# Modulation rows weighed on GpSimd, and a product order of its own at the start of units 2 to 14

## The chip, the cores and the metric

The kernel runs on one core of a Trainium2 chip. The metric is the device time of one execution in microseconds, as the median of several runs. Engines are named as the profile names them: PE (TensorE, with PEld for its weight loads), DVE (VectorE), ACT (ScalarE), POOL (GpSimd) and SP (SyncE, which here only issues DMAs).

## What is computed

A transformer block with adaptive layer norm, all in fp32: x is 2048 rows of 576 features. A condition vector c gives six rows of modulation, softmax attention with 32 heads of 18 features follows, then a gated feed-forward part with 4608 inner features.

```python
mod = (silu(c) @ w_mod).reshape(1, 6, 1, 576)
sa, ca, ga, sb, cb, gb = (mod[:, i] for i in range(6))
h = layernorm(x) * (1 + ca) + sa
q, k, v = split_heads(h @ wqkv)                  # 32 heads of 18
o = softmax(q @ k.T * 18 ** -0.5) @ v
x = x + ga * (merge_heads(o) @ wo)
h = layernorm(x) * (1 + cb) + sb
x = x + gb * ((sigmoid(h @ w_gate) * (h @ w_up)) @ w_down)
```

## The kernel before

**Stages.** First the layer norm and the projections of q, k and v (to about 240 us), then attention (to about 1600 us), then the feed-forward part. The change touches attention alone.

**Units and steps.** Attention runs over 32 units `u`. A unit is one half of the query rows (1024) and one pair of heads (`h` = 0, 1). It has 16 steps `kt`, one for each 128 keys. A step holds:
- four score products ("t", line 927): 128 keys by 512 queries, for two query chunks `c` and two heads, each followed by an exp on ACT (line 931) that takes the scores out of PSUM;
- four products for row maxima ("m", line 449, the generator `maxima`): 128 queries by 512 keys, for a unit that comes later. DVE reduces each (line 455). The order of the eight products of a block of 128 queries is in the table `MAXIMA`, as pairs (h, key chunk kc). In units outside `SINGLE` two of the eight are paired: product (0, 0) is made of the difference of two key chunks, ACT puts its relu into the tile `over` (line 458), and DVE later adds `over` to product (0, 1) and takes the maximum (line 460). The generator runs `LEAD` = 6 steps ahead, so that steps 0 and 1 of unit u make the fourth block (`qt` = 3) of unit u + 1;
- value products ("v", line 551, `values`): four products of 32 columns each, side by side, for the probabilities of two steps earlier. They sum into one PSUM tile `o` over a unit's 16 steps. A string such as "vmmttmmtvt" for even and "mtkttmwmmt" for odd steps gives the order; both calls of "v" fall into the even step.
- "k" (`taken`): after the last value product of a unit, ACT copies `o` to SBUF (line 565). That happens in step 1 of the next unit, and the next unit's first value product, in step 2, needs `o` free.
- "w": other work, in step 3 the four transposes of `outputs` (line 575), with a second ACT copy (line 590) and two POOL products (line 594). In step 13 `spread` writes the row maxima of a later unit into its query tile.

**What sets the order.** PE's order is the written one (`manual_schedule`). The other engines' orders are made by the framework's list scheduler when the program is built, so an instruction of theirs can be placed well ahead of where it is written. All score, maxima and helper products take their PSUM tiles from `bank()`, seven in rotation.

**Modulation.** `modulate(row, wm, pieces, takes)` makes two of the six rows at a time. `wm` holds five tiles of features (four of 128 and one of 64) by 2 x 576 columns of `w_mod`; `sc` is silu(c) by column. The weights of the products are `sc_b`, sc broadcast to 32 columns. For the later rows (`HALVES`) that is 5 x 2 x 2 = 20 products of 288 columns, summed over the five tiles; fp32 products have two rows in the profile, so 40 rows of line 124. Then DVE copies the sums to `row` (lines 130, 131), PE transposes it in three (line 142), and the results go to `mcol2` by DVE or to `ga_b` and `gb_b` by DMA (lines 148, 149). In unit 1 and in unit 3, after step 2, `load_mod` (lines 97, 98) loads the weights of two rows; after step 10 of the same unit `modulate` runs as a whole. The tiles `big`, `w0` and `w1` hold the weights and `row`.

**Others.** `downs` prepares `w_down` on POOL in the slots `w0` and `w1` (lines 826 to 848), one call every second step from step 64 (unit 4) to step 240 (unit 15); it needs `gb_b`.

Of the kernel before, what the change touches and what calls it, by code (L numbers as in the profile page):

```python
# [15 lines left out]
F32 = mybir.dt.float32  # L16
F32R = mybir.dt.float32r
AF = mybir.ActivationFunctionType
ALU = mybir.AluOpType
# [28 lines left out]

MAXIMA = ((1, 0), (0, 0), (1, 1), (0, 2), (1, 2), (0, 3), (0, 1), (1, 3))
SINGLE = (0, 1, 16, 17, 18, 19, 20, 27, 28, 29)  # L50
SIDES = ((0, 0), (0, 1), (1, 0), (1, 1))
TURNED = ((0, 1), (0, 0), (1, 1), (1, 0)), ((0, 1), (1, 1), (0, 0), (1, 0))
ORDERED = 7
# [5 lines left out]
def tile_block(ctx, tc, x_in, wqkv, wo, w_gate, w_up, w_down, c_in, w_mod, out):  # L59
# [41 lines left out]
    def ksize(t):  # L101
        return P if t < 4 else 64


    QUARTERS = (
        ((0, 0, 0, 384), (1, 0, 384, 192)), ((1, 192, DM, 64),),
    )
# [2 lines left out]
    def modulate(row, wm, pieces, takes):  # L110

        sc_b = row[:, 384:544].rearrange("p (t c) -> p t c", c=32)
        nc.vector.tensor_copy(sc_b, sc.unsqueeze(2).to_broadcast([P, 5, 32]))
        row = row[:, 0:384]
        pm = bank()
        for parts in pieces:
            for t in range(5):
                k = ksize(t)  # L120
                for v in range(2):
                    for g, to, f0, n in parts:
                        q = 32 * (2 * v + g)
                        nc.tensor.matmul(
                            pm[q : q + 32, to : to + n], sc_b[:k, t, :],
                            wm[t][:k, v * D + f0 : v * D + f0 + n],
                            start=t == 0, stop=t == 4, tile_position=(0, q),
                        )
        if pieces is HALVES:
            nc.vector.tensor_copy(row[:, 0:HALF], pm[:, 0:HALF])  # L130
            nc.vector.tensor_copy(
                row[:, HALF:384].rearrange("p (r c) -> p r c", c=32),
                pm[:, HALF - 32 : HALF].unsqueeze(1).to_broadcast([P, 3, 32]),
            )
        else:
            nc.vector.memset(row[:, 256:384], 0.0)
            nc.vector.tensor_copy(row[:, 0:256], pm[:, 0:256])
            for q in (0, 64):
                nc.vector.tensor_copy(row[q : q + 32, 256:384], pm[q : q + 32, 256:384])
        pt = bank()  # L140
        for b in range(3):
            nc.tensor.transpose(pt[:, b * P : (b + 1) * P], row[:, b * P : (b + 1) * P], ident)
        cols = pt[:, 0:384].rearrange("p (b q) -> p b q", q=P)
        for v, (dst, add) in enumerate(takes):
            if add is None:
                for g in range(2):
                    q = 64 * v + 32 * g
                    nc.sync.dma_start(gates[v : v + 1, g * HALF : (g + 1) * HALF], row[q : q + 1, 0:HALF])
                nc.sync.dma_start(dst, gates[v : v + 1, :].to_broadcast([P, D]))
            else:  # L150
                n = dst.shape[-1]
                nc.vector.tensor_scalar_add(dst[:, 0:3], cols[:, :, 64 * v], add)
                nc.vector.tensor_scalar_add(dst[:, 3:n], cols[:, 0 : n - 3, 64 * v + 32], add)
# [185 lines left out]
    with tc.tile_pool(name="ln", bufs=2) as ln:  # L339
        craw = early.tile([P, 5], F32, name="craw")  # L340
        nc.vector.memset(craw, 0.0)
        nc.sync.dma_start(craw[:, 0:4], c_in[0, 0:DM].rearrange("(t p) -> p t", p=P))
        nc.sync.dma_start(craw[0:64, 4:5], c_in[0, DM:D].rearrange("(p o) -> p o", o=1))
        nc.scalar.activation(sc, craw, AF.Sigmoid)
        nc.vector.tensor_mul(sc, sc, craw)

        def normalized(ch):
            xs = []
            for j in range(4):
                xt = ln.tile([P, 640], F32, name="x", bufs=8)  # L350
                nc.sync.dma_start(xt[:, :D], x_rows[:, ch * 4 + j, :])
                xs.append(xt)
            mv = ln.tile([P, 4, 2], F32, name="mv")
            rs = ln.tile([P, 4], F32, name="rs")
            for j, xt in enumerate(xs):
                ln_stats(ln, xt[:, :D], mv[:, j, :])
            ln_scales(ln, mv, rs)
            for j, xt in enumerate(xs):
                ln_apply(xt, xt[:, :D], mv[:, j, 0:1], rs[:, j : j + 1])
            return xs  # L360

        with tc.tile_pool(name="wmp", bufs=1) as wmp:
            zs = normalized(0)
            wm = wmp.tile([P, 5, 2 * D], F32, name="wm")
            wm = load_mod(wm[:, 0:4, :], wm[:, 4, :], 0)
            modulate(wmp.tile([P, 544], F32, name="mrow"), wm, QUARTERS, [(mcol[:, 1, :], 0.0), (mcol[:, 0, :], 1.0)])
        nc.gpsimd.memset(vaug, 1.0)
        wts = [load_qk([(0, P)]), load_qk([(D, P)])]
        with tc.tile_pool(name="wv0", bufs=1) as wvp:
            wv = load_v(wvp, 0)  # L370
            ln_transpose(ln, zs, hT, 0)
            zs = normalized(1)
            pls = []
            for ch in range(NCH):
                pls.append(project_qk([(wt, ch) for wt in wts]))
                if ch == 1:
                    key_differences(wvp, pls[0][:, :, 512:1024], pls[1][:, :, 512:1024], 0, P, 0)
                if ch + 1 < NCH:
                    ln_transpose(ln, zs, hT, (ch + 1) * 512)
                if ch + 2 < NCH:  # L380
                    zs = normalized(ch + 2)
                for t in (4 * ch, 4 * ch + 2):
                    project_v(wv, 0, t)
# [42 lines left out]
    def maxima():  # L426
# [4 lines left out]
        for u in range(UNITS):  # L431
# [5 lines left out]
            for i in range(8 * n):  # L437
                if last is not None and i == (9 if u == 1 else 8):
                    if u == 1:
                        spread(*last)  # L440
                    else:
                        state["spread"] = last
                qt = i // 8
                h, kc = MAXIMA[i % 8]
                rows = slice(64 * h, 64 * h + 3 * DH)
                paired = pairs and h == 0 and kc < 2
                at = NCH if paired and kc == 0 else kc
                sp = bank()
                nc.tensor.matmul(  # L449
                    sp, qs[rows, qt * P : (qt + 1) * P],  # L450
                    ks[rows, at * 512 : (at + 1) * 512], start=True, stop=True,
                )
                to = mx[:, h * n + qt, kc : kc + 1]
                if not paired:
                    nc.vector.tensor_reduce(to, sp, axis=AX.X, op=ALU.max)  # L455
                elif kc == 0:
                    over = small.tile([P, 512], F32, name="over", bufs=1)
                    nc.scalar.activation(over, sp, AF.Relu)
                else:
                    nc.vector.tensor_tensor_reduce(  # L460
                        out=over, in0=sp, in1=over, scale=1.0, scalar=LOWEST,
                        op0=ALU.add, op1=ALU.max, accum_out=mx[:, h * n + qt, 0:1],
                    )
                if i < 8 * n - 1:
                    yield
# [426 lines left out]
    for u in range(UNITS):  # L892
# [5 lines left out]
            Os.append(big.tile([P, 8, 640], F32, name="big"))  # L898
        for kt in range(NT):
            step = u * NT + kt  # L900
            turns["to"] = 64 + 4 * LEAD + 4 * (step + 1)
            kcols = slice(kt * P, (kt + 1) * P)
            plain = u in SINGLE
            sides = iter(SIDES if plain else TURNED[kt % 2])
            probs = [None] * 4
            for does in (("vtmmttmvtm", "tmttkwmtmm") if plain else ("vmmttmmtvt", "mtkttmwmmt"))[kt % 2]:
                if does == "m":
                    turn()
                elif does == "k":
# [21 lines left out]
                    state["exp"] = nc.scalar.activation(pr, sT, AF.Exp, scale=SCALE)  # L931
            pending.append((half, p, kt, probs))
            if u in (1, 3):
                if kt == 2:
                    a = big.tile([P, 8, 640], F32, name="big")
                    a = a.rearrange("p a b -> p (a b)")[:, 0 : 8 * D].rearrange("p (t c) -> p t c", t=4)
                    b = slots.tile([P, 2560], F32, name="w0")[:, 0 : 2 * D]
                    mods = load_mod(a, b, 1 + u // 2)
                    row = slots.tile([P, 2560], F32, name="w1")[:, 0:544]
                elif kt == 10 and u == 1:  # L940
                    modulate(row, mods, HALVES, [(ga_b, None), (mcol2[:, 1, :], 0.0)])
                elif kt == 10:
                    modulate(row, mods, HALVES, [(mcol2[:, 0, :], 1.0), (gb_b, None)])
            if 4 * NT <= step < FROM0 and step % 2 == 0:
                next(downs, None)
            if step == FROM0:
                for _ in downs:
# [471 lines left out]
```

## Time and profile before

| what | value |
|---|---|
| median of 3 runs | 2897.66 us (2895.02 to 2898.18) |
| profiled execution | 2895.19 us |
| its span, first to last instruction | 2893.2 us |
| PE busy | 2836.9 us |
| DVE, ACT, POOL busy | 2212.7, 1563.3, 644.6 us |
| products of the later modulation rows, L124, in units 1 and 3 | 2.74 us each, at 310.40 and 394.75 us |
| copies of `o` by ACT, L565 | 32, mean 608 ns |

A row of the chain of waits is "start us, length us, what ended last there"; "x8" is the number of instructions that are merged into it. In a timeline row stand start, length, engine, line, operation, output and inputs, and in brackets the idle time of the engine before it and what ended that. A row of the groups ends with busy us and mean ns, then idle us before them and who ended it.

### The profile page before, as it was taken

What the parts mean: (1) busy time and instruction counts of PE and PEld (TensorE: products, weight loads), DVE (VectorE), ACT (ScalarE), POOL (GpSimd) and SP (SyncE); (2) the same over time, 40 slices, a digit from 0 to 9 for tenths busy, and PEclk for the clock granted to TensorE, in tenths of its full rate; (3) what the DMA queues carried; (4) which work ended last, traced back from release to release, by engine and by line L of the source; (5) the groups of instructions that cost most, each with busy time, mean ns of one, the idle gap of its engine ahead of it and who ended that gap; (6) DMA issues with size and microseconds to landing.
All of it is one profiled execution on the core that took longest, in us unless ns stands there. A gap on an engine that the chain in (4) does not pass through costs nothing.

```text
span 2893.2 us, 46407 instructions
## 1 busy us (share of the span) xinstructions
PE 2836.9 (98%) x17141; PEld 1879.0 (65%) x17141; DVE 2212.7 (76%) x4055; ACT 1563.3 (54%) x2941; POOL 644.6 (22%) x829
## 2 busy tenths in 40 slices
PE   7999999999999999999999999999999999999998
PEld 5964333343444444444443788888888888888888
DVE  7287888888899988999983778888898555555555
ACT  2216889999987778998779322333333111111111
POOL 4023015444203111563101322222221100000000
PEclk9999999999999999999999999999999999999999
DMA  5344114333312111222215766667777845444453
GB/s 167 126 155 135 57 57 154 120 123 126 110 48 68 52 36 44 95 84 67 65 55 156 273 216 229 241 213 269 282 251 283 300 168 169 166 164 160 160 166 123
DMA packets 136386, 429.26 MB, mean 148 GB/s; under 512 B 19100, under 2 KB 55968, under 8 KB 123872
## 3 DMA queue, kind: packets, MB, share of 16 engines
q1 hardware_dynamic: 119664, 344.20, 35.2%
q0 software_dynamic: 16496, 82.10, 8.1%
q8 instruction: 135, 2.21, 0.3%
q14 instruction: 91, 0.75, 0.1%
HBM read 267.77 MB, written 157.95 MB: 147 GB/s over the span
## 4 chain that ended last, share of the span: by engine, by line
PE 89%; DVE 4%; ACT 4%; DMA 2%; issue 1%; SPq 0%; POOL 0%; DVEq 0%; POOLq 0%; ACTq 0%
PE x L1050 26%; PE o L551 17%; PE d L1096 15%; PE s L449 11%; PE s L927 11%; PE s L277 4%; ACT p L931 3%; PE s L688 2%; PE s L328 2%; DVE mx L455 1%; PE s L575 1%; DMA ws<-w 1%; DVE w L1040 0%; DVE Oa L1100 0%; DMA wm<-in_w_mod_dram 0%
## 5 line engine op out<-in xcount | busy, mean ns | idle before, releaser
L455 DVE TENSOR_REDUCE mx<-s 128x1 f32<-128x512 f32 x1696 | 1076.5, 684 | 122.2 <-PE s L449 108.4
L931 ACT ACTIVATE p<-s 128x512 f32<-128x512 f32 x2048 | 1068.8, 610 | 147.4 <-PE s L449 80.4
L449 PE MATMUL s<-k,q 54*128 54x512 f32 x1920 | 607.4, 450 | 13.0 <-ACT p L931 6.0
L551 PE MATMUL o<-p,vaug 128*32 128x512 f32 x4096 | 554.1, 606 | 0.4 <-ACT p L931 0.4
L927 PE MATMUL s<-q,k 56*128 56x512 f32 x1920 | 551.4, 425 | 0.7 <-DMA q<-mrows 0.2
L1096 PE MATMUL d<-wd,hh 128*128 128x288 f32 x2304 | 460.9, 295 | 3.0 <-DVE Oa L1100 2.8
L927 PEld LDWEIGHTS s<-q,k 56*128 56x128 f32 x1920 | 260.1, 186 | 293.5 <-DVE mx L455 183.8
L449 PEld LDWEIGHTS s<-k,q 54*128 54x128 f32 x1920 | 273.4, 184 | 250.3 <-ACT p L931 172.0
L1096 PEld LDWEIGHTS d<-wd,hh 128*128 128x128 f32 x2304 | 373.4, 188 | 9.7 <-DVE Oa L1100 3.7
L1050 PE MATMUL x<-k,w 128*128 128x512 f32 x1512 | 357.6, 391 | 2.4 <-ACT w L1031 2.4
L1100 DVE TENSOR_TENSOR Oa<-Oa,d 128x288 f32<-128x288 f32 x576 | 256.3, 454 | 134.2 <-PE d L1096 128.3
L1096 PE MATMUL d<-wd,hl 128*128 128x288 f32 x1152 | 340.3, 295 | 0.0
L1050 PEld LDWEIGHTS x<-k,w 128*128 128x128 f32 x1512 | 282.7, 188 | 59.3 <-ACT w L1031 2.6
L1050 PE MATMUL x<-big,w 128*128 128x512 f32 x1008 | 235.6, 390 | 0.7 <-DVE u L1338 0.7
L1050 PE MATMUL x<-w,w 128*128 128x512 f32 x1008 | 235.7, 390 | 0.0
L1096 PEld LDWEIGHTS d<-wd,hl 128*128 128x128 f32 x1152 | 216.2, 188 | 0.0
L1050 PEld LDWEIGHTS x<-big,w 128*128 128x128 f32 x1008 | 188.8, 188 | 40.4 <-DVE u L1338 1.4
L1050 PEld LDWEIGHTS x<-w,w 128*128 128x128 f32 x1008 | 187.1, 188 | 36.7
L551 PEld LDWEIGHTS o<-p,vaug 128*32 128x32 f32 x4096 | 83.4, 108 | 163.8 <-issue 152.0
L1059 ACT ACTIVATE sg<-x 128x512 f32<-128x512 f32 x36 | 21.5, 598 | 299.2 <-PE x L1050 299.1
L1061 ACT ACTIVATE u<-u 128x512 f32<-128x512 f32 x72 | 45.4, 631 | 239.6 <-DVE u L1338 215.0
L1104 POOL DMA_DIRECT2D out_dram<-Oa x16 | 8.7, 544 | 602.2 <-DVE Oa L1100 602.2
(218 smaller groups left out, 2953.9 us busy)
## 6 DMA issues: line engine op xcount, KB each, us to landing
ws<-w SPq DMA_DIRECT2D x126, 640.0 KB
w<-ws SPq DMA_DIRECT2D x126, 640.0 KB
wd<-wds SPq DMA_DIRECT2D x36, 1152.0 KB
k<-kd SPq DMA_DIRECT2D x60, 360.0 KB
wds<-w POOLq DMA_DIRECT2D x18, 1152.0 KB, 4.5
k<-kd SPq DMA_DIRECT2D x60, 180.0 KB
w<-in_B_w_down_dram POOLq DMA_DIRECT2D x18, 576.0 KB, 4.4
q<-qd SPq DMA_DIRECT2D x64, 144.0 KB
```

Of the source, the lines that this page charges most:

```text
L277: nc.tensor.matmul(acc, w, hT[:, t, cols], start=n == 0, stop=n == len(ts_) - 1)
L328: nc.tensor.matmul(acc[:, 0:HALF], hT[:, k, rows], w, start=n == 0, stop=n == len(ts_) - 1,)
L449: nc.tensor.matmul(sp, qs[rows, qt * P : (qt + 1) * P], ks[rows, at * 512 : (at + 1) * 512], start=True, stop=True,)
L455: nc.vector.tensor_reduce(to, sp, axis=AX.X, op=ALU.max)
L551: nc.tensor.matmul(acc[32 * j : 32 * j + 32, :], vaug[:, kt, (2 * p + h) * VW : (2 * p + h) * VW + 32], probs[2 * c + h], start=kt == 0, s ...
L688: nc.tensor.matmul(acc[:, :HALF], a, w, start=i == 0, stop=i == len(ts_) - 1)
L927: nc.tensor.matmul(sT, ks[rows, kcols], qs[rows, c * 512 : (c + 1) * 512], start=True, stop=True)
L931: state["exp"] = nc.scalar.activation(pr, sT, AF.Exp, scale=SCALE)
L1050: nc.tensor.matmul(acc[v], w[:, v, a, :], X[s][:, b, :], start=first and n == 0, stop=n == 6, skip_group_check=not first,)
L1061: nc.scalar.activation(t[:, 0:512], t[:, 0:512], AF.Sigmoid)
L1096: nc.tensor.matmul(acc[:, :HALF], a[:, f, rows], w[:, f, cols], start=n == 0, stop=n == 5)
L1100: nc.vector.tensor_add(Oa[:, t, cols], Oa[:, t, cols], acc[:, :HALF])
```

## The change

1. `weigh(wm)`: POOL scales each feature tile by its column of `sc` and adds tiles 1 to 4 to tile 0, in ten pieces, one for each tile and row. `modulate` then needs one tile: its weights are ones, and 4 products are left of 20. It is now a generator with a break before the transposes.
2. `load_mod` is written after step 0 of units 1 and 3, `weigh` after steps 5 to 14 of them. `modulate` is written after step 2 (products and copies) and step 4 (transposes and what follows) of units 2 and 4. `downs` begins 8 steps later.
3. In steps 0 and 1 of units 2 to 14 the products have an order of their own. Step 0 has "vmmmttmttmvm" instead of "vmmttmmtvt", step 1 "kttmtmt" instead of "mtkttmwmmt": six maxima in step 0 and two in step 1 in place of four and four, and in step 0 only one product follows the second "v". `STARTED` orders the scores, and `FIRST` the maxima, with relu's product (0, 0) as the first and (0, 1) as the fourth.

```diff
+FIRST = ((0, 0), (1, 0), (0, 2), (0, 1), (1, 1), (1, 2), (0, 3), (1, 3))
+STARTS = tuple(range(2, 15))
+STARTED = ((0, 0), (0, 1), (1, 1), (1, 0)), ((0, 0), (0, 1), (1, 0), (1, 1))
...
+    def weigh(wm):
+
+        for t in range(5):
+            k = ksize(t)
+            for c0 in (0, D):
+                part = wm[t][:k, c0 : c0 + D]
+                nc.gpsimd.tensor_scalar(part, part, sc[:k, t : t + 1], 0.0, op0=ALU.mult, op1=ALU.add)
+                if t:
+                    whole = wm[0][:k, c0 : c0 + D]
+                    nc.gpsimd.tensor_tensor(whole, whole, part, op=ALU.add)
+                yield
...
-        nc.vector.tensor_copy(sc_b, sc.unsqueeze(2).to_broadcast([P, 5, 32]))
+        last = len(wm) - 1
+        if last:
+            nc.vector.tensor_copy(sc_b, sc.unsqueeze(2).to_broadcast([P, 5, 32]))
+        else:
+            nc.vector.memset(sc_b[:, 0, :], 1.0)
...
-            for t in range(5):
+            for t in range(last + 1):
...
-                            start=t == 0, stop=t == 4, tile_position=(0, q),
+                            start=t == 0, stop=t == last, tile_position=(0, q),
...
+        yield
         pt = bank()
...
-                h, kc = MAXIMA[i % 8]
+                h, kc = (FIRST if pairs and qt == 3 and u - 1 in STARTS else MAXIMA)[i % 8]
...
-            turns["to"] = 64 + 4 * LEAD + 4 * (step + 1)
+            turns["to"] = 64 + 4 * LEAD + 4 * (step + 1) + (2 if kt == 0 and u in STARTS else 0)
...
-            sides = iter(SIDES if plain else TURNED[kt % 2])
+            starts = u in STARTS and kt < 2 and not plain
+            sides = iter(SIDES if plain else (STARTED if starts else TURNED)[kt % 2])
...
-            for does in (("vtmmttmvtm", "tmttkwmtmm") if plain else ("vmmttmmtvt", "mtkttmwmmt"))[kt % 2]:
+            order = ("vtmmttmvtm", "tmttkwmtmm") if plain else ("vmmttmmtvt", "mtkttmwmmt")
+            if starts:
+                order = ("vmmmttmttmvm", "kttmtmt")
+            for does in order[kt % 2]:
...
             if u in (1, 3):
-                if kt == 2:
+                if kt == 0:
...
+                    weighed = weigh(mods)
-                elif kt == 10 and u == 1:
-                    modulate(row, mods, HALVES, [(ga_b, None), (mcol2[:, 1, :], 0.0)])
-                elif kt == 10:
-                    modulate(row, mods, HALVES, [(mcol2[:, 0, :], 1.0), (gb_b, None)])
-            if 4 * NT <= step < FROM0 and step % 2 == 0:
+                elif kt >= 5:
+                    next(weighed, None)
+            elif u in (2, 4) and kt in (2, 4):
+                takes = [(ga_b, None), (mcol2[:, 1, :], 0.0)] if u == 2 else [(mcol2[:, 0, :], 1.0), (gb_b, None)]
+                if kt == 2:
+                    weighed = modulate(row, mods[:1], HALVES, takes)
+                next(weighed, None)
+            if 4 * NT + 8 <= step < FROM0 and step % 2 == 0:
                 next(downs, None)
```

More of the change, by code (lines that the diff above doesn't have):

```diff
@@ L365, in tile_block @@
             wm = load_mod(wm[:, 0:4, :], wm[:, 4, :], 0)
-            modulate(wmp.tile([P, 544], F32, name="mrow"), wm, QUARTERS, [(mcol[:, 1, :], 0.0), (mcol[:, 0, :], 1.0)])
+            for _ in modulate(
+                wmp.tile([P, 544], F32, name="mrow"), wm, QUARTERS, [(mcol[:, 1, :], 0.0), (mcol[:, 0, :], 1.0)]
+            ):
+                pass
         nc.gpsimd.memset(vaug, 1.0)
```

## The prediction

> **What bounds the kernel now.** I read the page first, then the chain of waits from 200 to 420 us, where the change works, then the timelines of TensorE, ScalarE and VectorE there, the groups of GpSimd, and two windows.
>
> ```profile
> PE 2836.9 (98%) x17141; PEld 1879.0 (65%) x17141; DVE 2212.7 (76%) x4055; ACT 1563.3 (54%) x2941; POOL 644.6 (22%) x829
> ```
>
> By the page PE has no room. For the attention that is only half the truth: its matmuls are issued in a written order, one product has to wait for a free PSUM bank (seven in rotation), and ScalarE or VectorE empties it. The chain shows this, step by step. Columns: start, length, what.
>
> ```profile
> 296.84 1.00 PE o L551 x8
> ...
> 301.95 1.00 PE o L551 x8
> ...
> 307.07 1.00 PE o L551 x8
> ...
> 310.40 2.74 PE s L124 x40
> ...
> 315.89 0.99 PE o L551 x8
> ...
> 333.43 0.99 PE o L551 x8
> ...
> 361.35 1.00 PE o L551 x8
> ...
> 364.99 0.61 ACT p L931
> ...
> 366.22 1.00 PE o L551 x8
> ...
> 371.31 1.00 PE o L551 x8
> ...
> 373.45 0.99 PE o L551 x8
> ...
> 376.59 1.00 PE o L551 x8
> ...
> 381.47 1.00 PE o L551 x8
> ...
> 386.33 1.00 PE o L551 x8
> ...
> 391.19 1.00 PE o L551 x8
> ...
> 394.75 2.74 PE s L124 x40
> ...
> 400.34 0.99 PE o L551 x8
> ...
> 415.56 1.00 PE o L551 x8
> ```
>
> The rows of L551 are the clock: each even step kt begins with such a burst of value products and has a second one. The rows quoted at 296.84, 301.95, 307.07 and 315.89 are the first bursts of steps 6, 8, 10 and 12 of unit 1; 333.43 is the second burst of step 2 in unit 2; 361.35, 366.22, 371.31, 376.59 and 381.47 are step 14 of unit 2 and steps 0, 2, 4 and 6 of unit 3; then come steps 8 and 10, L124, and step 12 at 400.34; 415.56 is step 2 of unit 4. A quiet pair of steps takes 366.22 - 361.35 = 4.87 us. The pair of steps 0 and 1 takes 371.31 - 366.22 = 5.09, that of 2 and 3 5.28. Two pairs stand out: 307.07 to 315.89 is 8.82, against 5.12 before it, and 391.19 to 400.34 is 9.15, against 4.86 before it. Both hold the modulation (L124).
>
> **Part 1: the two long pauses go.** Units 1 and 3 lose all of modulate(): 8.82 - 5.12 = 3.70 and 9.15 - 4.86 = 4.29, together **-7.99 us**.
>
> **Part 2: what comes in for them on TensorE.** Unit 2 and unit 4 get, after step 2, four products with ones in place of twenty. The 40 rows of L124 took 2.74, so 8 rows take 0.55. To that comes the change between tile shapes, for which I need the next view.
>
> ```profile
> 366.15 1.07 PE L551 MATMUL o<-p,vaug 128*32 128x512 f32 x8
> 367.14 0.51 PE L449 MATMUL s<-k,q 54*128 54x512 f32 x2
> 367.48 0.41 PE L927 MATMUL s<-q,k 56*128 56x512 f32 x2
> 367.72 0.41 PE L449 MATMUL s<-k,q 54*128 54x512 f32 x2
> 367.95 0.40 PE L927 MATMUL s<-q,k 56*128 56x512 f32 x1
> 368.28 1.06 PE L551 MATMUL o<-p,vaug 128*32 128x512 f32 x8
> ...
> 370.81 0.50 PE L449 MATMUL s<-k,q 54*128 54x512 f32 x1 [0.32 <-ACT p L931]
> ...
> 371.24 1.07 PE L551 MATMUL o<-p,vaug 128*32 128x512 f32 x8
> ```
>
> Score products follow each other in pairs at 0.24 (367.48 to 367.72), but 0.34 after a burst (367.14 to 367.48) and 0.33 before one (367.95 to 368.28). Going in and out of another tile shape thus costs about 0.2, and the inserted piece 0.75. Does anything hide it? In the chain every piece of the pair of steps 2 and 3 of unit 3 belongs to PE (371.31 to 376.59), so no: 0.75. Without the switch it would be 0.55. The two copies of the sums into `row` go to VectorE and nobody waits for them before step 4: nothing, or 0.3 if they push a reduction that a bank waits for. After step 4 three transposes follow: they stood 0.52 in the old pause.
>
> ```profile
> 397.51 0.47 DVE w L130
> ...
> 398.12 0.52 PE s L142 x3
> ```
>
> The old pause also held the copy that they waited for (0.61 from 397.51 to 398.12); now the copy is two steps old. In quiet pairs PE waits for ScalarE somewhere (364.99), so part of 0.52 is hidden: 0.35, between 0.1 and 0.6. Per unit that is 1.1, for two units **+2.2 us** (1.3 to 3.0).
>
> **Part 3: GpSimd.** Each chunk gets ten scalings and eight additions of 576 columns.
>
> ```profile
> L740 POOL TENSOR_TENSOR t<-t 128x512 f32<-128x512 f32 x12 | 15.3, 1279 | 1.2 <-DVE t L800 1.1
> L778 POOL TENSOR_SCALAR z<-Oa,mv,rs 128x128 f32<-128x128 f32 x48 | 37.7, 791 | 56.1 <-PE s L798 44.8 <-DVE rs L179 11.0
> ```
>
> An addition is 1.28 x 576/512 = 1.44, eight are 11.5. A scaling lies between 0.79 (all of L778 fixed) and 3.56 (all of it per element), so a chunk takes 19 to 47 us. I take the low side, since L778 has scattered 128-column pieces and two column operands. The Trainium skill (GPSIMD Engine Reference, "Performance versus the Vector engine") has about 1.8 cycles an element at 1.2 GHz for the best one-input loop, an estimate of 0.86 us for 576; no run here has that form, and by it a chunk would take 20 us.
>
> The first chunk's sums are due when TensorE ends step 2 of unit 2, near 334.4 (the burst of 333.43 and 0.99). The program writes the work from step 5 of unit 1 on; its end is near 296.8, and 37.6 us are left. It will probably start long before, because only TensorE's order is fixed by hand, and the others take what is ready:
>
> ```profile
> 247.90 0.31 DVE L115 COPY w<-sc 128x160 f32<-128x160 f32 x1
> ```
>
> This copy belongs to the modulation of step 10 in unit 1, and it ran 62 us ahead of L124. So I cost GpSimd at nothing. What covers it: GpSimd has no other work between unit outputs here. And beside VectorE:
>
> ```profile
> 341.45:361.35 19.90, 19.70 (x134) 7.96 (x137) 18.08 (x35) 18.92 (x38) 0.00 (x0) 1.00 0.00 1
> 461.00:481.00 20.00, 19.83 (x136) 7.83 (x128) 18.01 (x36) 19.06 (x38) 13.12 (x22) 1.00 0.34 116
> ```
>
> The columns are PE, PEld, DVE, ACT, POOL busy, the granted clock and DMA. With GpSimd idle VectorE was busy for 18.08 us, with GpSimd at 13.12 us for 18.01: it is not slowed. [...]
>
> The loads move from step 2 to step 0 on SyncE's queue; the second must wait for the ones-products at 334.4 and needs to be there only for unit 3. `downs` begins four calls later: 74 calls of the 84 that remain, so it still ends before unit 15. Both nothing; if the load blocked the queue, the query and key loads for two units ahead would be late first.
>
> **Part 4: the new order of steps 0 and 1, thirteen times.** ScalarE and VectorE in the old pair:
>
> ```profile
> 367.68 1.89 DVE L455 TENSOR_REDUCE mx<-s 128x1 f32<-128x512 f32 x3 [0.21 <-PE s L449]
> ```
>
> ```profile
> 367.71 0.60 ACT L458 ACTIVATE over<-s 128x512 f32<-128x512 f32 x1 [0.16 <-PE s L449]
> 368.20 1.57 ACT L931 ACTIVATE p<-s 128x512 f32<-128x512 f32 x3
> 369.64 0.62 ACT L565 COPY oT<-o 128x512 f32<-128x512 f32 x1
> 370.10 2.61 ACT L931 ACTIVATE p<-s 128x512 f32<-128x512 f32 x5
> 372.80 0.60 ACT L458 ACTIVATE over<-s 128x512 f32<-128x512 f32 x1
> ```
>
> Ten ScalarE instructions start every 0.48 (368.20 to 369.64 is three of them): 4.81 with the first at 0.49. The pair takes 372.80 - 367.71 = 5.09, so 0.28 is idle. TensorE in turn waits 0.32 for an exp's bank at 370.81, because the copy stands in front.
>
> Now I walk the new order, with 0 at the first burst of step 0. Relu's product and (1,0) start at 0.99, (0,2) at 1.33, two scores at 1.57, (0,1) and a score at 1.80. Each start is taken from the old rows: first reduction 367.68, relu 367.71, both less 366.15, so 1.53 and 1.56. The eighth and ninth product need their banks: the relu holds one for 0.60, the reduction for at least a third of 1.89, so both come free near 2.2, and 0.33 after the ninth product the second burst may start. The second burst goes from 2.6 to 3.6, 0.5 later than before. ScalarE meanwhile has its relu at 1.56 and exps at 2.05, 2.53, 3.01, 3.49, so the copy at 3.97 finds the burst done. TensorE issues (1,2) and the scores of step 1 from 3.6 to 4.4, each bank being free by then, and the next burst at 4.74; its PSUM tile is free at 4.6, a margin of 0.15. ScalarE: copy 3.97, exps 4.45 to 5.89, free at 6.37; the next relu's product is there at 6.30. No wait is left, the pair takes 4.81, and it gains 0.28 (0.35 seen from TensorE). Thirteen units: **-3.6 us**, between -4.6 and, if the late second burst returns it, 0.
>
> **The sum.** -7.99 + 2.2 - 3.6 = -9.4 us. The profiled execution took 2895.19 (span 2893.2); it becomes 2885.8. The median of the runs lies 2.5 above that execution, so I forecast **2888.3**. A measurement here can tell 0.2%, 5.8 us.
>
> **The rivals.** *The order gives nothing*: the 0.28 comes back because the second burst is 0.5 later. For it: the margin is 0.15. Against: ScalarE alone needs 4.81. Then -5.8: 2891.9.
> *The copy of `o` falls behind two exps of step 1*: the next burst waits to 4.74 + 0.96 - 0.15 = 5.55, the pair loses 0.46 instead, +6.0 for thirteen, and the sum is about 0: 2897.9. Against it: the old trace puts the copy ahead of exps that the program writes earlier (369.64 before 370.10).
> *The sums come late* (the other side): GpSimd keeps the order of writing and a scaling costs 3.56. TensorE, in fixed order, stops in front of four products, and all behind it. Chunk 1: 296.8 + 47 = 343.8 against 334.4, 9.4 late. Chunk 2: from the end of step 5 in unit 3 (381.47) + 47 = 428.5 against step 2 of unit 4, at 415.56 + 3.1 (as 371.31 to 374.44) - 4.29 = 414.4: 14.1 late. With the other terms +14: 2911.7. It decides from 37.6 us a chunk, that is 2.6 us a scaling. Against it: the early copy above, and an idle GpSimd.
>
> **How the numbers follow.** Forecast 0.69, order without gain 0.17, copy late 0.06, sums late 0.06, 0.02 for the rest. The forecast's own range goes from -11.3 (both low ends) to -7; the run-to-run spread of 3 us is laid on it. The range 2884.5 to 2894 takes in the forecast and the first rival, and leaves the other two out. Faster by over 0.2%: nearly all of the forecast and half of the first rival, 0.73. Same: the other half, the late copy and a little, 0.19. Slower: 0.08.
>
> **What would show it.** Right: pairs at step 10 of units 1 and 3 near 5.1 and 4.87; the pair of steps 2 and 3 of units 2 and 4 near 6.0 and that of steps 4 and 5 near 5.2; steps 0 and 1 of units 2 to 14 near 4.8, with relus that wait for nothing; GpSimd's scalings ahead of unit 2. Wrong: TensorE waiting for POOL in front of the ones-products, or for the copy L565 in front of a first burst, or pairs of steps 0 and 1 still at 5.1.

## The result and the profile after

| | before | after |
|---|---|---|
| median | 2897.80 us (2895.02 to 2899.16, 10 runs) | 2890.39 us (2886.99 to 2893.10, 10 runs) |
| profiled execution | 2895.19 us, span 2893.2 | 2886.99 us, span 2885.2 |

The ratio is 0.9973, with an interval of 0.9963 to 0.9983. The change saves 7.4 us; 9.4 were forecast. The profiled execution of after is the fastest of its ten, which matters below.

By the page of after, PE has 64 matmul rows fewer (17077 for 17141) and is busy for 2833.0 us; POOL has 36 instructions more (865 for 829) and is busy for 680.2.

The chain of waits of after (start, length, what). L574 is the burst that was L551, L143 the products with ones, L162 the transposes of `row`, L954 the scores, L472 the maxima.

```profile
304.89 0.99 PE o L574 x8
...
310.01 1.00 PE o L574 x8
...
325.19 0.99 PE o L574 x8
...
328.38 0.43 PE s L954
328.81 0.62 PE s L143 x8
329.43 0.43 PE s L472
...
331.58 0.99 PE o L574 x8
...
334.69 0.43 PE s L954
335.12 0.48 PE s L162 x3
...
337.30 1.00 PE o L574 x8
...
386.90 1.00 PE o L574 x8
...
391.76 0.99 PE o L574 x8
...
523.66 1.00 PE o L574 x8
...
526.41 1.00 PE o L574 x8
...
528.54 0.99 PE o L574 x8
...
533.88 0.99 PE o L574 x8
```

- **Pauses.** 304.89 to 310.01 is the pair of step 10 in unit 1: 5.12 where 8.82 stood. 386.90 to 391.76 is that of unit 3: 4.86 where 9.15 stood. Over both that is -7.99.
- **Pieces.** 325.19, 331.58 and 337.30 are steps 2, 4 and 6 of unit 2. The pairs take 6.39 and 5.72; before, 5.28 and 4.87. The new order gives 0.06 back in the first (below), so the pieces cost 1.05 and 0.86. Unit 4 has the same, so together 3.8.
- **Order.** 523.66, 528.54 and 533.88 are steps 0, 2 and 4 of unit 7. Steps 0 and 1 take 4.88 for 5.09, steps 2 and 3 take 5.34 for 5.28.

PE's waits for exps, as the view of waits adds them up (total us, times, longest), first of before, then of after:

```profile
PE s L449 <- ACT p L931: 10.2, 19, 4.2
```

```profile
PE s L472 <- ACT p L958: 6.0, 7, 4.2
```

There are twelve waits and 4.2 us fewer: the wait of 0.32 that the prediction read at 370.81 stood in each of the thirteen units (0.32 to 0.37) and now stands in none. But a pair got shorter by 0.23 only; the order experiments say why.

GpSimd in the groups of 250 to 355 us, by form (busy us, mean ns):

```profile
L117 POOL TENSOR_TENSOR big<-big 128x576 f32<-128x576 f32 x12 | 16.8, 1416 | 0.0
L114 POOL TENSOR_SCALAR big<-big,sc 128x576 f32<-128x576 f32 x16 | 11.7, 744 | 1.5 <-DMA big<-in_w_mod_dram 1.4
```

And GpSimd's timeline:

```profile
253.04 2.91 POOL L114 TENSOR_SCALAR big<-big,sc 128x576 f32<-128x576 f32 x4
...
335.03 2.91 POOL L114 TENSOR_SCALAR big<-big,sc 128x576 f32<-128x576 f32 x4 [1.44 <-DMA big<-in_w_mod_dram]
```

Ten scalings at 0.74 and eight additions at 1.42 make 18.8 us a chunk. The first chunk begins at 253.04, 76 us ahead of L143, and its last group of scalings at 299.10. The second begins at 335.03, as soon as its load has landed, some 75 us ahead of need. Nobody waits for it. VectorE beside it, in the view of one line (the reductions L478), first 335 to 351 us with GpSimd busy for 15.97 of 16 us, then 353 to 369 us with GpSimd idle (min/median/max ns):

```profile
L478 DVE TENSOR_REDUCE mx<-s x19: 655/686/693, 336.1 to 350.6; 128x1 f32<-128x512 f32 x19
...
L478 DVE TENSOR_REDUCE mx<-s x21: 680/682/692, 352.5 to 369.0; 128x1 f32<-128x512 f32 x21
```

**The balance of the two profiled executions.** In the sums by unit, from the first bursts in both traces, units 1 to 15 are 5.8 shorter: -7.99 + 3.8 - 2.2 + 0.7, and 0.1 in small differences. The -2.2 is the order as it is in a quiet unit (13 x 0.17); the 0.7 are two units, 5 and 12, whose steps 0 and 1 did not gain but took 5.32 and 5.11. The rest of the span's -8.0 lies where the change has nothing: attention starts 1.5 earlier (241.84 for 243.37), unit 0 -0.65, unit 20 -1.44, other late units and the tail +1.5. In the experiments attention starts anywhere from 241.8 to 246.9, also in kernels whose beginning is that of after. Unit 20 takes 46.8, 48.2 or 49.7, whatever was edited. So the change itself is worth 5.8 us in the traces. Against the medians, -7.4, that leaves 1.6 open; the interval of the ratio, 4.9 to 10.7 us, holds both.

### The profile page after: what moved, and what is told of

It reads as the page before. It is cut to its first block, busy times and chain, and to the rows that moved or that the text cites. A ratio compares the mean times of both kernels' runs of the same rounds, so it can differ in the third digit from the quotient of the medians.

```text
span 2885.2 us, 46301 instructions
## 1 busy us (share of the span) xinstructions
PE 2833.0 (98%) x17077; PEld 1878.1 (65%) x17077; DVE 2212.5 (77%) x4055; ACT 1563.1 (54%) x2941; POOL 680.2 (24%) x865
## 4 chain that ended last, share of the span: by engine, by line
PE 91%; DVE 3%; ACT 3%; DMA 1%; issue 1%; POOL 0%; SPq 0%; ACTq 0%; POOLq 0%; DVEq 0%
PE x L1081 27%; PE o L574 17%; PE d L1127 15%; PE s L472 12%; PE s L954 11%; PE s L297 4%; ACT p L958 2%; PE s L711 2%; PE s L348 2%; DVE mx L478 1%; PE s L598 1%; DVE w L1071 0%; DVE Oa L1131 0%; PE d L1266 0%; DMA wm<-in_w_mod_dram 0%
## 5 line engine op out<-in xcount | busy, mean ns | idle before, releaser
L478 DVE TENSOR_REDUCE mx<-s 128x1 f32<-128x512 f32 x1696 | 1076.9, 685 | 117.7 <-PE s L472 100.0
L472 PE MATMUL s<-k,q 54*128 54x512 f32 x1920 | 606.0, 450 | 8.2 <-ACT p L958 1.8
L954 PE MATMUL s<-q,k 56*128 56x512 f32 x1920 | 554.5, 425 | 1.1 <-DVE mx L478 0.4
L574 PE MATMUL o<-p,vaug 128*32 128x512 f32 x4096 | 553.1, 605 | 0.4 <-ACT p L958 0.4
L954 PEld LDWEIGHTS s<-q,k 56*128 56x128 f32 x1920 | 264.3, 185 | 290.6 <-DVE mx L478 175.4
L472 PEld LDWEIGHTS s<-k,q 54*128 54x128 f32 x1920 | 272.6, 184 | 250.2 <-ACT p L958 151.4
L574 PEld LDWEIGHTS o<-p,vaug 128*32 128x32 f32 x4096 | 83.3, 108 | 161.6 <-issue 145.3
```

Of the source, the lines that this page charges most:

```text
L472: nc.tensor.matmul(sp, qs[rows, qt * P : (qt + 1) * P], ks[rows, at * 512 : (at + 1) * 512], start=True, stop=True,)
L574: nc.tensor.matmul(acc[32 * j : 32 * j + 32, :], vaug[:, kt, (2 * p + h) * VW : (2 * p + h) * VW + 32], probs[2 * c + h], start=kt == 0, s ...
L954: nc.tensor.matmul(sT, ks[rows, kcols], qs[rows, c * 512 : (c + 1) * 512], start=True, stop=True)
```

## The experiments

Two things were to be explained: why the pieces cost 3.8 and not 2.2, and why the order gave 2.2 at best and not 3.6. Theory A has the pieces priced by their place among PE's tile shapes, and the start of a unit bound by ScalarE; its rivals have the price elsewhere. Each text below says in numbers what they expect of its run. The table gathers what was measured; "units 1 to 15" is the sum of the pairs of steps there against the profiled execution of before, which leaves out what happens in the rest of the program.

| run | median us (before beside it) | ratio | units 1 to 15 |
|---|---|---|---|
| the change | 2890.39 (2897.80) | 0.9973 [0.9963, 0.9983] | -5.8 |
| e1_weigh_only | 2894.14 (2898.40) | 0.9984 [0.9975, 0.9993] | -3.3 |
| e2_order_only | 2894.40 (2898.40) | 0.9985 [0.9976, 0.9994] | -2.2 |
| e3_beside_bursts | 2888.46 (2898.40) | 0.9968 [0.9956, 0.9979] | -7.8 |
| e4_extra_act | 2898.01, one run | | +0.9 |
| e5_beside_downs6 | 2889.87 (2898.64) | 0.9969 [0.9960, 0.9979] | -8.2 |
| e6_double_ones | 2891.33, one run | | -4.7 |
| e7_between_pairs | 2892.16, one run | | -6.6 |
| e8_old_extra_act | 2902.40, one run | | +5.8 |
| e9_changed_again | 2889.44 (2898.91) | 0.9971 [0.9960, 0.9981] | -5.7 |
| e10_moved_again | 2885.11 (2898.91) | 0.9962 [0.9949, 0.9976] | -8.2 |

### One half at a time

```diff
# e1_weigh_only, against the changed kernel
-STARTS = tuple(range(2, 15))
+STARTS = ()
```

> The changed kernel with the old product order in every unit (STARTS empty). My theory, from the pairs of steps of the changed kernel: the long pauses go (-3.71 and -4.28) and the new pieces cost 1.05 + 0.86 in units 2 and 4, so attention is 4.2 us shorter and the pairs of steps 0 and 1 are 5.09 again; the piece in steps 2 and 3 then makes them 5.28 + 1.05 = 6.33. Rival, that the order carries most of the change: under 2 us faster than before. Rival, that the early time (the first value burst 1.5 us earlier) comes from the change: it is there here too; if it is the load of the first weights that varies between executions, it may be absent.

```diff
# e2_order_only, against the kernel before: FIRST, STARTS and STARTED and their uses alone
+            if starts:
+                order = ("vmmmttmttmvm", "kttmtmt")
...
```

> The kernel before with the new order of steps 0 and 1 in units 2 to 14, and nothing else of the change. My theory: each of the thirteen pairs of steps 0 and 1 goes from 5.09 to 4.87 and the pair of steps 2 and 3 after it gives 0.06 back, so attention is 13 x 0.17 = 2.2 us shorter; the unit 5, which did not gain in the changed kernel (5.32), gains here, because GpSimd's transfers of w_down stand elsewhere. As I predicted it, with ScalarE's starts at 0.48, it would be 3.6 us. Rival, that the order gives nothing of its own: 0 us, and pairs at 5.09.

Both halves gain by themselves. In e1 the pauses go (-3.70 and -4.28), the pieces cost 1.07 + 0.87 in unit 2 and 1.03 + 0.85 in unit 4, and steps 0 and 1 stay at 5.09. So the pieces do not cost 3.8 because of the new order. Unit 5's steps 0 and 1 take 6.04, 0.95 more than before; e5 comes back to that. In e2 all thirteen pairs take 4.86 or 4.87, units 5 and 12 too, and in all but one of the thirteen units steps 2 and 3 give 0.04 to 0.09 back: 0.17 a unit, -2.2 in all. The stalls of units 5 and 12 are thus not the order's own: that of unit 5 is in e1 too, that of unit 12 in neither half alone. The sums, -3.3 and -2.2, make -5.5 of the -5.8 that both together have.

### Where the pieces stand in PE's order

```diff
# e3_beside_bursts: products behind the first burst of step 2,
# transposes behind those of outputs() in step 3
                     if step >= LAG:
                         values()
+                    if u in (2, 4) and kt == 2 and probs == [None] * 4:
+                        takes = ...
+                        weighed = modulate(row, mods[:1], HALVES, takes)
+                        next(weighed, None)
...
                         outputs()
+                        if u in (2, 4):
+                            next(weighed, None)
...
```

> The changed kernel with its pieces of modulation at other places of the same units: the four products right behind the first value burst of step 2, the transposes right behind the four transposes of outputs() in step 3. Theory A, that a piece costs its own time (0.62 and 0.48) and, where it stands between two score products, about 0.43 because these no longer run side by side: the pair of steps 2 and 3 grows by 0.62 + 0.48 = 1.1 in all and that of steps 4 and 5 is 4.87 again, so the two units together lose 2.2 instead of 3.8, 1.6 us faster than the changed kernel. Theory B, that a piece costs about 0.95 wherever it stands, for the change of tile shape or for the PSUM bank it holds: no difference, 3.8. Theory C, that the transposes now wait for VectorE's copies: the pair of steps 2 and 3 grows by 1.5 or more.

```diff
# e7_between_pairs: each piece behind "vmmtt" of steps 2 and 4
+            for place, does in enumerate(order[kt % 2]):
+                if u in (2, 4) and kt in (2, 4) and place == 5:
...
+                    if kt == 2:
+                        weighed = modulate(row, mods[:1], HALVES, takes)
+                    next(weighed, None)
...
```

> The changed kernel with both pieces written between two complete pairs of products: behind the first five entries (vmmtt) of steps 2 and 4 instead of at their ends. Theory A, that at the end of a step a piece splits a pair that would run side by side (0.23) and changes the tile shape twice (0.2): without the split the pair of steps 2 and 3 grows by 0.62 + 0.2 = 0.82 instead of 1.05, and that of steps 4 and 5 by about 0.65 instead of 0.86. Theory B, that the change of shape alone is the fixed part (0.43): 1.05 and 0.86 again. Theory C, that only the piece's own time counts unless it splits a pair: 0.62 and 0.48.

```diff
# e6_double_ones: each product with ones issued twice
+                        for twice in range(1 if last else 2):
                             nc.tensor.matmul(
...
```

> The changed kernel with each of the four products with ones issued twice (eight products, sixteen rows; the sums are then twice what they should be or, where the second replaces the first, the same). Theory A, that a piece costs its rows at full length and a fixed part: the pairs of steps 2 and 3 of units 2 and 4 grow by 0.52 (8 x 0.065) over the 6.38 of the changed kernel, to 6.9, and all others stay. Theory B, that the first 0.3 of a bubble hides part of a piece, so that the marginal price is above the mean price: more than 0.62. Theory C, that part of it is hidden: under 0.3.

The chains of waits of e3, e7 and e6 at steps 2 to 6 of unit 2, in this order:

```profile
328.56 1.00 PE o L574 x8
329.55 0.48 PE s L143 x8
...
333.83 0.33 PE s L162 x3
...
334.93 1.00 PE o L574 x8
...
339.79 1.00 PE o L574 x8
```

```profile
329.22 0.99 PE o L574 x8
...
330.88 0.62 PE s L143 x8
331.50 0.43 PE s L472 x2
...
335.30 0.99 PE o L574 x8
...
336.97 0.48 PE s L162 x3
337.44 0.43 PE s L472 x2
...
340.85 0.99 PE o L574 x8
```

```profile
328.01 1.00 PE o L575 x8
...
331.63 1.13 PE s L144 x16
...
334.90 0.99 PE o L575 x8
```

In e6 eight rows more make the piece 0.51 longer (1.13 for 0.62) and the pair of steps 2 and 3 of unit 2 0.50 longer than the 6.39 of after (6.89, 328.01 to 334.90), as its Theory A had it: every row costs its full time, nothing hides any of it. Of 0.62 then 0.51 is the rows' own and 0.11 is the entry, the price of coming in from products of another tile shape. In e3, behind a burst of the same 128x32 tiles, the entry is gone (0.48), and behind transposes that are there anyway the three of L162 take 0.33 for 0.48. The pairs take 6.37 and 4.86; less 5.28 + 0.06 and 4.87 that is 1.02 for both pieces together (1.1 in unit 4) instead of 1.91.

e7 separates the rest. Behind "vmmtt" both pieces have the same own time as after (0.62 and 0.48), and the two products that follow side by side take 0.43 again where such a pair in a quiet stream takes 0.24: 0.19 for the way back. That makes 0.62 + 0.19 = 0.81 and 0.48 + 0.19 = 0.67; the pairs show 6.08 - 5.28 - 0.06 = 0.74 (329.22 to 335.30) and 5.55 - 4.87 = 0.68 (to 340.85), near the 0.82 and 0.65 of its Theory A. After has 1.05 and 0.86. The difference, 0.3 and 0.2, is what the written place adds: after "vmmttmmtvt" the last score stands alone between the second burst and the piece (328.38 and 334.69 in the chain of after, 0.43 and no partner), and its partner, the first maximum of the next step, pays 0.43 again behind it. Between the place of the change and that of e3 lie 0.8 to 0.9 us a unit. The Trainium skill (TensorEngine Tiling (Array Packing), section "Key Properties") says that a change of the tiling mode drains TensorE. It gives no price; the chains here agree and price it at 0.11 in and 0.19 out.

### What bounds steps 0 to 3

```diff
# e4_extra_act: the changed kernel, and one ScalarE copy more in step 1 of units 2 to 14
             nc.scalar.copy(oT, acc)
+            if u in STARTS:
+                nc.scalar.copy(bgp.tile([P, 512], F32, name="spare"), oT)
```

> The changed kernel with one more ScalarE copy (128 x 512, from the copy of o to a spare tile) behind the copy of o in step 1 of units 2 to 14. Theory A, that with the new order ScalarE alone bounds steps 0 and 1: each pair of steps 0 and 1 grows by one ScalarE start, 0.48, from 4.87 to 5.35. Theory B, that TensorE's own work or the banks bound them and ScalarE has room: it grows by less than 0.2.

```diff
# e8_old_extra_act: the same copy in the kernel before
             nc.scalar.copy(oT, acc)
+            if 2 <= u <= 14:
+                nc.scalar.copy(bgp.tile([P, 512], F32, name="spare"), oT)
```

> The kernel before with one more ScalarE copy (128 x 512, from the copy of o to a spare tile) behind the copy of o in step 1 of units 2 to 14: the same addition that made steps 0 to 3 of the changed kernel longer by 0.50 a unit. Theory A, that the old order left ScalarE 0.28 idle in steps 0 and 1: the copy fills that and steps 0 to 3 together grow by about 0.2, to 10.57. Theory B, that ScalarE was as full in the old order: they grow by 0.48 to 0.50, to 10.86.

ScalarE's timeline in unit 7, of after and of e4 (start, length, instruction):

```profile
525.13 0.60 ACT L481 ACTIVATE over<-s 128x512 f32<-128x512 f32 x1
525.66 2.07 ACT L958 ACTIVATE p<-s 128x512 f32<-128x512 f32 x4
527.59 0.62 ACT L588 COPY oT<-o 128x512 f32<-128x512 f32 x1
528.05 2.12 ACT L958 ACTIVATE p<-s 128x512 f32<-128x512 f32 x4
530.04 0.63 ACT L481 ACTIVATE over<-s 128x512 f32<-128x512 f32 x1
```

```profile
533.47 0.60 ACT L481 ACTIVATE over<-s 128x512 f32<-128x512 f32 x1
...
536.87 0.67 ACT L590 COPY spare<-oT 128x512 f32<-128x512 f32 x1
...
538.82 0.69 ACT L481 ACTIVATE over<-s 128x512 f32<-128x512 f32 x1
```

The chains of waits, the first bursts of steps 0, 2 and 4 of the same unit in e4, then in e8:

```profile
532.01 1.00 PE o L574 x8
...
536.87 1.00 PE o L574 x8
...
542.71 1.00 PE o L574 x8
```

```profile
534.23 1.00 PE o L551 x8
...
539.32 1.00 PE o L551 x8
...
544.92 1.00 PE o L551 x8
```

The copy does not lengthen steps 0 and 1 on PE: they stay at 4.86 (532.01 to 536.87), so ScalarE's starts, which e4's Theory A named, are not what sets that pair. PE's timeline of after shows what does:

```profile
525.78 0.49 PE L954 MATMUL s<-q,k 56*128 56x512 f32 x1
525.91 0.50 PE L472 MATMUL s<-k,q 54*128 54x512 f32 x1
...
529.47 0.50 PE L472 MATMUL s<-k,q 54*128 54x512 f32 x2
```

The eighth product behind the first burst (525.78) gets its bank when the relu is done (525.13 + 0.60). The ninth (525.91) follows the first reduction (525.16, and about 0.69 long). So the two no longer run side by side, and the second burst comes at 526.41. From there to the next relu's product (529.47) PE stands in no further wait.

ScalarE in turn is nearly full in after, but not quite. No bracket stands between the relus, yet its ten starts take 4.91 (525.13 to 530.04), not 4.81. The second relu comes 0.57 behind its product, as it does in before with ScalarE idle in front of it (372.24 to 372.80); in e4, where ScalarE is late, it comes 1.03 behind (537.79 to 538.82). So some 0.05 is a wait for PE. Another 0.04 lies behind the first relu, whose exp follows after 0.53 where before has 0.49; these runs do not say why.

With one copy more the ten starts and the copy take 5.35 (533.47 to 538.82), and the copy's price, 0.50 a unit, stands in steps 2 and 3, which take 5.84. PE runs up to seven banks ahead of ScalarE and pays later. So Theory A had the price right and the place wrong.

e8 adds the same copy to the old order. It costs 0.32 there, between the two numbers of its text, and again all of it in steps 2 and 3 (5.60 for 5.28). Over steps 0 to 3 the old order takes 10.37 (366.22 to 376.59 in before's chain), the new one 10.22 (523.66 to 533.88), and with the extra copy they take 10.69 (e8) and 10.70 (e4). Once ScalarE has one more instruction, the order no longer matters. Without it the old order leaves ScalarE 0.16 more room over these four steps than the new one: the copy costs 0.32 there and 0.48 here. The new order gains by using up that room. Whether a better order could still get the 0.05 that the second relu waits, no run tries. e8's execution also has 1.17 in unit 5, as e1 had 0.95.

### Unit 5, and both moves together

In before, e2, e5 and e10 steps 0 and 1 of unit 5 take as long as those of the other units; in all other runs they take 0.4 to 1.2 longer. The unit's first scores, from 443.6 on in after, read the row maxima: four DMAs of 4 KB, which SyncE issues from 439.33 on, the last at 441.48. Beside them GpSimd's queue has two bulk transfers of `downs`, a store of 1152 KB issued at 440.90 and a load of 576 KB at 443.32. The store in GpSimd's timeline of after, then of before:

```profile
440.90 0.61 POOL L871 DMA_DIRECT2D wds<-w  x1 [0.30 <-POOL w L866]
```

```profile
448.51 0.59 POOL L848 DMA_DIRECT2D wds<-w  x1 [0.30 <-POOL w L843]
```

Before has the same two transfers at nearly the same place, and no stall. There the store is issued 0.20 behind the last of the row maxima (448.31), in e2 1.2 behind it. In all eight executions with the stall it is issued 0.2 to 0.6 ahead of the last one. That holds for e8 too, where `downs` begins as in before, so the stall goes with the order of issue and not with the start of `downs` as such. Why the store holds the last row maxima up is not shown.

```diff
# e5_beside_downs6, e10_moved_again: e3, with downs two steps earlier
-            if 4 * NT + 8 <= step < FROM0 and step % 2 == 0:
+            if 4 * NT + 6 <= step < FROM0 and step % 2 == 0:
```

> The changed kernel with both pieces of modulation beside other work of their own shape (products behind the first burst of step 2, transposes behind those of outputs()), and with downs begun at step 70 instead of 72. My theory: the first pair of unit 5, which took 5.32 to 5.41 in the kernels with downs at 72, was held by the row maxima's DMA standing behind GpSimd's store of the first w_down block; two steps earlier that store is over in time, and the pair takes 4.87 like the others. So 0.5 us below the kernel that has the moved pieces alone, about 10 us below the kernel before. Rival, that something else holds unit 5 (a wait on VectorE): 5.3 or more again.

e9 is the changed kernel once more, to stand beside e10 on one chip.

> The changed kernel once more, on the same chip and against the same runs as the next one. By the pairs of steps: 5.7 us below the kernel before (7.99 for the pauses, less 3.8 for the pieces, and 1.6 for the order).

> The changed kernel with its pieces moved beside work of their own shape and downs begun at step 70, on the same chip as the one before this. By the pairs of steps: 2.2 us below the changed kernel (2 x 0.85 for the pieces, 0.5 for the first pair of unit 5). Rival, that the moved pieces only shift a wait past attention: the same time as the changed kernel.

PE's waits for the row maxima (total, times, longest) in e9, then in e10:

```profile
PE s L954 <- DMA q<-mrows: 0.7, 2, 0.4
```

```profile
PE s L960 <- DMA q<-mrows: 0.2, 1, 0.2
```

With `downs` two steps earlier the store goes 4.6 ahead of the last row maxima and lands within 0.2 of its issue. Unit 5's pair then takes 4.86 in e5 and in e10, and one of the two waits is gone; the other, of 0.2, the kernel before has too. e1, e4 and e8, which had the longest pairs, show this wait with 0.9, 0.7 and 1.2 as the longest. In after itself the view puts the stall down to a VectorE reduction (0.4), and e6 and e7 do not name the DMA either; that it stood behind the stall there too is read from the order of issue and from the other runs, not shown. Unit 12's 0.25, in after, e6, e7 and e9 but in no other run, has no cause that these runs show.

By pairs, units 1 to 15 of e10 are 2.5 shorter than those of e9: 0.87 and 0.80 from the place of the pieces, 0.52 and 0.25 from units 5 and 12. The medians, 2885.11 and 2889.44, are 4.3 apart; 1.45 more of it is unit 20 in the profiled executions. The intervals overlap, so that e10 beats the change rests on the pairs, which agree in e5 and e10; that it beats the kernel before is plain from 0.9962 [0.9949, 0.9976].

## Why the prediction was right, and where its sizes were off

- **Part 1** held to the hundredth: -7.99 forecast and measured, because both ends of each pause stood in the trace of before as quiet neighbours.
- **Part 2 was too small:** 2.2, with bounds of 1.3 to 3.0, against 3.8. Its first term, 0.75, agrees with a piece between two complete pairs (0.74 in e7), though its parts do not: 0.55 for the rows and 0.2 for the tile shapes stand against 0.51 and 0.30. It left out that the written place splits a pair (0.3). Its second term, 0.35, came from "part of 0.52 is hidden". Nothing was hidden: 0.68 in e7, and 0.86 in the place of the change.
- **Part 3:** GpSimd at nothing was right, with a chunk at the low end of 19 to 47 us. A scaling took 0.74, below the fixed 0.79 of the nearest row. By the Trainium skill (GPSIMD Engine Reference, "Performance versus the Vector engine", 1.8 cycles an element at 1.2 GHz) it was an estimate of 0.86; the measurement decides. VectorE's reductions beside it differ by 4 ns (686 and 682). `downs` at nothing was wrong by half a microsecond in both executions of the changed kernel: it ends in time, as argued, but its store moved from 0.2 behind the last row maxima of unit 5 to 0.4 to 0.6 ahead of it, and of SyncE's queue the prediction asked only for the query and key loads.
- **Part 4 was too large:** -3.6 against -2.2 alone and -1.6 with units 5 and 12. The walk had the mechanism right: the wait of 0.32 is gone, the second burst comes later, and the copy finds it done. The failed step is the bank of the ninth product. The walk has it come free near 2.2 with that of the eighth, from a reduction that holds it for a third of 1.89, 0.63; the reduction takes 0.69, and the ninth product starts 0.13 behind the eighth. That puts the second burst at 2.75 and not 2.6, the next first burst at 4.88 and not 4.74, and the next relu waits for its product, where the walk had ScalarE as the last. And the sum was taken over steps 0 and 1 alone; 0.06 of it goes back in steps 2 and 3, where e4 shows a late ScalarE to be paid. The bank is read from the rows; no run moves it.
- **The rivals.** "The order gives nothing" was wrong in the pairs, though two units behave like it. The copy fell behind nothing, and the sums were never late.
- **The sum.** The errors of Parts 2 and 4, +1.6 and +2.0, point the same way, so by its own steps the forecast was 3.6 too low. The time came out only 2.1 above it, because the medians hold the 1.6 that units 1 to 15 of the traces do not. That is luck, as far as these runs show. Right in sign and range, the forecast was less right in its terms than the total suggests.

## What to carry to other kernels

Price a piece that is put into a written matmul order by its neighbours: it pays its own rows, the change of tile shape on both sides, and a pair of small products that it splits; next to a burst of the same shape or beside the same kind of work it costs half. When a reordering removes a wait, ask how much room the engine behind the wait has over the whole stretch until the next idle time: here that room (0.16), and not the wait (0.32), is what was gained. And when background transfers shift by even a microsecond, look at every small DMA beside them, and at which of the two is issued first.

## What was not expected of the hardware

- Going into four 32-column tiles from the score products cost 0.11 us and coming back 0.19; splitting a side-by-side pair another 0.2 to 0.3 (e3, e6, e7).
- A relu of 128x512 starts 0.54 to 0.57 us behind the start of its product at the earliest seen here (524.59 to 525.13 and 529.47 to 530.04 in after, 367.14 to 367.71 in before).
- Row maxima of 4 KB on SyncE's queue made PE wait for up to 1.2 us (e8) when a store of 1152 KB on GpSimd's queue was issued 0.2 to 0.6 us ahead of the last of them. Issued 0.2 us behind it (before), the same store made no wait.
- GpSimd at 15.97 of 16 us busy, mostly with two-input additions, changed VectorE's reductions by 0.6%.
